# Windowed attention with a highway layer: q and k in half as many transfers, the bias by another queue, one part of q ahead of a weight matrix

## The chip, the cores and the metric

The kernel runs on one core of one Trainium2 chip. A core has five engines that run their own instruction streams in order: TensorE (PE, matmuls; its weight loads are shown as PEld), VectorE (DVE), ScalarE (ACT), GpSimd (POOL) and SyncE (SP). SP, ACT and POOL also issue DMA transfers; all of these run on the core's 16 DMA engines. The metric is the device time of one execution in microseconds (us), lower is better.

## The reference

The inputs are q, k and v of shape (4 batches, 8 heads, 768 positions, 64), and a highway layer's weights w_h and w_t (512 x 512) and bias b_t. Everything is float32 and the output is 3072 x 512.

```python
scores = scale * np.matmul(q, k.transpose(0, 1, 3, 2))
keep = (pos[None, :] < 4) | ((rel >= 0) & (rel < 128))    # 4 sinks, a window of 128
a = softmax(np.where(keep, scores, -1e9))
x = np.matmul(a, v)  # heads side by side: (4 * 768, 512)
H = np.maximum(x @ w_h, 0.0)
T = 1.0 / (1.0 + np.exp(-(x @ w_t + b_t)))
out = T * H + (1.0 - T) * x
```

A query sees itself, the 127 keys before it, and the first four keys of its sequence.

## The kernel before

The work is cut into N = 24 tiles of 128 positions, six for each batch, and each tile carries all eight heads. Tile n needs the keys of its own 128 positions against the queries of tiles n and n + 1, so that one exponential serves both tiles that see these keys.

**Loading.** q and k come as float32 and are needed as float16, cut into segments: three thirds of 256 positions for batches 0 and 1, two halves of 384 for batches 2 and 3. `load_part(b, i, g, which)` (L113) loads, for a group g of two heads, one segment i of q (which = 0) or k (which = 1) into 32 of the 128 partitions of `nat`, with a cast on the way, by POOL's queue; `load_rows` (L122) calls it for the four groups. So each segment of q or k is four transfers of 32 x 2 rows. The first two thirds of q of batch 0 come uncast, as `first`, by the queues of SP and ACT (L180, L197), and are cast by an engine. DVE's `transpose_qk` (L126, L133) turns `nat` into `tr`, from which the products are made. v comes by SP (`load_v`, L137) as float32 with eight buffers, and is cast by `cast_v` (L149) on DVE for tiles 0 to 5 and on POOL from 6 on. w_h and w_t come by POOL with a cast; so does the bias b_t, into `brow`, four rows of 512 at partitions 0, 32, 64 and 96, where a small matmul (L372) adds it to the gate's sum.

**A tile.** `opening` (L387) writes the masks (L309) and the products (L334) of tile n into `ps_s`, of which there is one, with the bias (L372) and the sinks (L380) of earlier tiles in between. ACT takes the exponential into `E` (`expo`, L422). `values(n - 1)` (L433, L436) multiplies E by v, DVE divides (`norm`, L444 and L446) into X, PE transposes X (L462), ACT copies it (L467). Then come the gate (`gate`, L472; `tanh`, L480), the hidden layer (L493), and the combination on DVE (L506, L511) and POOL or DVE (L517), and SP stores the tile.

**What sets the order.** Each engine's order is that of the program text (`_keep_traced_order`, L24). The loop over n (L597) interleaves the stages of tiles n, n - 1 and n - 2. What is loaded, cast and turned in which iteration is written out by hand: `units` (L548) says which segments are turned in iteration n, `loads` (L560) which parts are issued on POOL, `v_at` (L564) which tiles of v are issued on SP; below iteration 6 a load of v waits for the last product of that iteration's scores (`after`, L611). The bf16 and fp16 matmuls at the start and in iterations 0 and 1 (`idle`, L521) work on zeros. On POOL the order at the start is: the first third of k (four parts), the second third of k, the bias (L206), w_t (L207), the last third of q, the last third of k, the copy and product of the sink values (L291, L292), one part of q of batch 1, w_h (L593), and then the loop's.

Of the kernel before, what the change touches and what calls it, by code (L numbers as in the profile page):

```python
# [11 lines left out]
FP32 = mybir.dt.float32  # L12
# [25 lines left out]
def kernel(  # L38
# [13 lines left out]
    P = 128  # L52
    pe, act, dve, pool, sp = nc.tensor, nc.scalar, nc.vector, nc.gpsimd, nc.sync

    B, H, S, D = q.shape
# [5 lines left out]
    NT, DM = out.shape  # L61
# [4 lines left out]
    G = 4  # L66
    HG = H // G
# [4 lines left out]
    const = ctx.enter_context(tc.tile_pool(name="const", bufs=1))  # L72
# [22 lines left out]
    def gate_of(n, part):  # L95
# [6 lines left out]
    segments = [thirds if b < 2 else halves for b in range(B)]  # L102
    nat = [[data.tile([P, 2, HG, nt // 32, D], FP16, tag=f"nat{b}_{t0}", name=f"nat{b}_{t0}")
            for t0, nt in segments[b]] for b in range(B)]
# [5 lines left out]
    def v_of(n):  # L110
        return vt[n % 8]

    def load_part(b, i, g, which, into=None, engine=pool):  # L113

        t0, nt = segments[b][i]
        into = nat[b][i][:, which] if into is None else into
        engine.dma_start(  # L117
            out=into[32 * g:32 * g + 32].rearrange("p hg m d -> p hg (m d)"),
            in_=(q, k)[which][b, :, t0:t0 + nt, :].rearrange(
                "(hg g) (r m) d -> g r hg (m d)", g=G, m=nt // 32)[g])  # L120

    def load_rows(b, i, which, gs=range(G)):  # L122
        for g in gs:
            load_part(b, i, g, which)

    def transpose_qk(b, i, which, hgs=slice(0, HG)):  # L126

# [9 lines left out]
    def load_v(n, after=None):  # L137
        b, t = divmod(n, NC)
        V32[n] = work.tile([P, H, D], FP32, tag="V32", name="V32", bufs=8)
        ins = sp.dma_start(out=V32[n],  # L140
                           in_=v[b, :, t * P:(t + 1) * P, :].transpose([1, 0, 2]))
        if after is not None:
            tc.add_manual_dep(
                ins.ins, after.ins.name,
                mybir.DependencyInfo(
                    mybir.DependencyClass.Sync, mybir.DependencyReason.DATA),
                reason="behind the loads needed first")

    def cast_v(n, engine):  # L149
        engine.tensor_copy(out=v_of(n)[:, :, 0:D], in_=V32[n])  # L150
# [14 lines left out]
    wh = const.tile([P, KC, DM], FP16, tag="wh")  # L165
    wt = const.tile([P, KC, DM], FP16, tag="wt")
    brow = const.tile([P, DM], FP16, tag="brow")
    ones = const.tile([P, P], FP16, tag="ones")
    vs32 = const.tile([P, B, D + 1], FP32, tag="vs32")
    vmask = const.tile([P, H], FP32, tag="vmask")  # L170
# [7 lines left out]
    first = [data.tile([P, HG, SEG // 32, D], FP32, tag=f"first{i}", name=f"first{i}")  # L178
             for i in range(2)]
# [3 lines left out]
    def load_sinks(b, gs=range(G)):  # L183
        for g in gs:
            hs = slice(G * (g // 2), G * (g // 2) + G)
            sp.dma_start(out=vs32[16 * g:16 * g + 16, b, 0:D], in_=v[b, hs, 0:NSINK, :])

    dve.memset(zeros, 0.0)
    dve.memset(brow, 0.0)
    pool.iota(away, pattern=[[1, K2]], base=0, channel_multiplier=-4,  # L190
              allow_small_or_imprecise_dtypes=True)
    load_rows(0, 0, 1)
    for g in range(G):
        pool.iota(vmask[32 * g:32 * g + 32, :], pattern=[[-NSINK, H]], base=0,
                  channel_multiplier=1, allow_small_or_imprecise_dtypes=True)
# [3 lines left out]
    load_v(0)  # L199
    load_v(1)  # L200
    load_sinks(0, range(2, G))
    make_identity(nc, ident)
    load_rows(0, 1, 1)


    pool.dma_start(out=brow[0:P:32, :], in_=moe_b_t.unsqueeze(0).to_broadcast([G, DM]))  # L206
    pool.dma_start(out=wt, in_=moe_w_t.rearrange("(kc p) of -> p kc of", p=P))  # L207
    load_rows(0, 2, 0)
    load_rows(0, 2, 1)

    dve.memset(ebias, _EXP_BIAS)
    for g in range(1, G):
        m = away[32 * g:32 * g + 32, :]
# [76 lines left out]
    def sink_values(b):  # L290
        pool.tensor_copy(out=vs32[64:P, b, 0:D], in_=vs32[0:64, b, 0:D])  # L291
        pool.tensor_tensor(  # L292
            out=vs[b], in0=vs32[:, b].unsqueeze(1).to_broadcast([P, H, D + 1]),
            in1=vmask.unsqueeze(2).to_broadcast([P, H, D + 1]), op=ALU.mult)
# [123 lines left out]
    def expo(n):  # L418
        c = n % NC
        nq = 2 if c + 1 < NC else 1  # L420
        E[n] = work.tile([P, G, HG, 2 * P], FP16, tag="E", name="E")
        act.activation(out=E[n][:, :, :, 0:nq * P], in_=ps_s[:, :, :, 0:nq * P],  # L422
                       func=AF.Exp, bias=ebias, scale=SCALE)
# [97 lines left out]
    def idle(count):  # L521
        for _ in range(count):
            pe.matmul(ps_h, lhsT=zeros[:, 0:P], rhs=zeros, start=True, stop=True,
                      skip_group_check=True)
# [24 lines left out]
    for b in range(1, B):  # L549
# [3 lines left out]
        else:  # L553
            at = (9, 10, 10, 11, 12, 13, 13, 14) if b == 2 else (15, 16, 16, 17, 18, 19, 19, 20)
            for u, n in enumerate(at):
                i, which, hg = u // 4, u // 2 % 2, u % 2
                units.setdefault(n, []).append((b, i, which, slice(hg, hg + 1)))
    issues = [(b, i, g, which) for b in range(1, B) for i in range(len(segments[b]))
              for which in range(2) for g in range(G)][2 * G:]
    loads = {}  # L560
    for n, count in zip(range(2, 18), [4] * 4 + [3] * 7 + [1] + [3] * 3 + [1]):
        loads[n] = [issues.pop(0) for _ in range(count)]
    assert not issues
    v_at = {1: (2,), 2: (3,), 3: (4,), 4: (5,), 5: (6, 7), 6: (8, 9)}  # L564
# [24 lines left out]
    cast_v(0, dve)  # L589
    sink_keys(0, dve)  # L590
    sink_values(0)
    load_rows(1, 0, 0, range(1))
    pool.dma_start(out=wh, in_=moe_w_h.rearrange("(kc p) of -> p kc of", p=P))  # L593

    idle(18)
    last = N - 1
    for n in range(last):  # L597

        nb, n1 = n - 2, n - 1
        joined = n < 5 or n >= 7  # L600
        before = (n1 if 0 <= n1 < N else None, nb if nb >= 0 else None)
        if n < N:
            after = opening(n, *before) if joined else scores(n)
            expo(n)
            if n in (4, 5):
                gate_value(n - 4)
            if n > NC and n % NC == NC - 1:
                gate_value(n - 3)
            for m in v_at.get(n, ()):
                if m < N:  # L610
                    load_v(m, after if n < 6 else None)  # L611
            if n % NC == 3 and n // NC + 1 < B:
                load_sinks(n // NC + 1)
        if 5 <= n <= 6:
            hidden(1 if n == 5 else 3)
        if n == 0:
            idle(5)
        if not joined:
            opening(None, *before)
        if 0 <= n1 < N:  # L620
            values(n1)
        if n >= 6:
            cast_v(n, pool)
        if NC <= n < N and n % NC == 0:
            sink_keys(n // NC)
        if n == 2:
            load_rows(1, 0, 0, range(1, G))
            load_rows(1, 0, 1)
        for b, i, g, which in loads.get(n, ()):
            load_part(b, i, g, which)  # L630
        if n > NC and n % NC == 1:
            sink_values(n // NC)

        done = list(completed.get(n, ()))
        if n == 6:
            while done:
                complete(done.pop(0))
        turn = list(units.get(n, ()))
        if 5 <= n <= 6:
            diff(1 if n == 5 else 3)  # L640
        if 0 <= n1 < N:
            norm(n1)
        if n == 3:
            transpose_qk(0, 2, 1, slice(1, 2))
        if n == 2:
            transpose_qk(0, 2, 0)
        if n == 1:
            transpose_qk(0, 1, 1)
        if 0 < n < 4:
            cast_v(n, dve)  # L650
        if n == 2:
            transpose_qk(0, 2, 1, slice(0, 1))
        for unit in turn if n != 4 else ():
            transpose_qk(*unit)
        if n == 5:
            cast_v(n, dve)

        if nb >= 0:
            gate(nb)
            tanh(nb)  # L660
        if n == 4:
            hidden(0)
            diff(0)
            transpose_qk(*turn.pop())
            cast_v(n, dve)
        if n == 5:
            gate_value(2)
            hidden(2)
        if n == 1:
            idle(3)  # L670
        if 6 <= n <= N:
            hidden(nb, range(KC // 2))
        if 0 <= n1 < N:
            x_transpose(n1)
            if n in sinks_at:
                sink_scores(*sinks_at[n])
            x_copy(n1)
            if n in sinks_at:
                sink_expo(*sinks_at[n])
            if nb >= N - 4:  # L680
                gate_value(nb)
        if 6 <= n <= N:
            hidden(nb, range(KC // 2, KC))
        if n in ahead:
            gate_value(ahead[n], pool)
        if n == last - 1:
            cast_v(last, pool)
        for m in done[:-1]:
            complete(m)
        if n == 5:  # L690
            diff(2)
        if 6 <= n <= N:
            diff(nb)
        for m in done[-1:] if n < last - 1 else ():
            complete(m)
# [83 lines left out]
```

## Time and profile before

| what | us |
|---|---|
| median of three runs | 108.66 |
| lowest and highest run | 107.71 and 108.89 |
| the profiled execution, its time | 108.7 |
| its span, first to last instruction | 106.7 |
| TensorE busy in the span | 94.7 |
| VectorE, ScalarE, GpSimd busy | 86.4, 80.8, 83.8 |

In the lines below, a group or a timeline row names the engine, the line of the kernel, the operation, what it writes and reads, and how often; a bracket at the end of a row of the timeline says how long the engine was idle before it and what ended that. A row of the waits has the waiting engine and line, what it waited for, the total in us, the times, and the longest. A row of the DMA issues has the queue, the number of issues, KB of each and the median us from issue to landing. The two slices lines show tenths of busy time in 40 equal parts of the span.

### The profile page before, as it was taken

To read this page: it belongs to the slowest core of one execution; us is meant where nothing else is said; L and a number is where in the kernel's file an instruction comes from. 1 tells how busy PE (TensorE), PEld (TensorE's weight loads), DVE (VectorE), ACT (ScalarE), POOL (GpSimd) and SP (SyncE) were. 2 spreads that over 40 slices of the span, in tenths; PEclk is the share of its full clock that TensorE was granted. 3 is DMA by queue.
4 is the path that set the end of the run, shared out by engine and by line. 5 is a ranking of instruction groups with operands and counts; after the bars stand their busy time and mean duration, and the time that the engine had idled before them with its cause. 6 is when DMAs were issued, how large, how long until landed. Compare 5 with 4: busy or idle time off the path is not lost. (4 is left out here: it accounts for less than half of the span.)

```text
span 106.7 us, 4672 instructions
## 1 busy us (share of the span) xinstructions
PE 94.7 (89%) x1960; PEld 53.0 (50%) x1960; DVE 86.4 (81%) x188; ACT 80.8 (76%) x105; POOL 83.8 (79%) x139
## 2 busy tenths in 40 slices
PE   5976885889999997799999999999999999999930
PEld 2323452466454654456655467555655565465610
DVE  6988854657796798879998987899889979998960
ACT  3387677689776788778869997897789978986750
POOL 6898729937849999999999999999777829778000
PEclk9999999999999999999999999999999999999999
DMA  2999999999999998879999998999997763252523
GB/s 77 217 256 213 160 202 239 143 188 210 236 216 202 218 157 244 149 176 268 197 234 270 259 237 211 206 244 200 228 266 186 200 179 115 104 198 83 215 84 114
DMA packets 36388, 20.81 MB, mean 195 GB/s; under 512 B 27020, under 2 KB 32912, under 8 KB 36368
## 3 DMA queue, kind: packets, MB, share of 16 engines
q1 hardware_dynamic: 29216, 13.31, 46.7%
q0 software_dynamic: 6848, 6.82, 41.5%
q10 hardware_dynamic: 304, 0.39, 1.2%
q8 instruction: 15, 0.25, 1.0%
q14 instruction: 5, 0.04, 0.1%
HBM read 21.05 MB, written 6.29 MB: 256 GB/s over the span
## 5 line engine op out<-in xcount | busy, mean ns | idle before, releaser
L422 ACT ACTIVATE E<-ps_s,ebias 128x2048 f16<-128x2048 f32 (+1 forms) x24 | 43.8, 1825 | 11.2 <-PE ps_s L334 10.0
L133 DVE STREAM_TRANSPOSE tr<-nat 128x384 f32<-128x384 f32 (+2 forms) x29 | 26.4, 936 | 2.5 <-DMA nat<-in_q_dram 1.4
L493 PE MATMUL ps_h<-wh,XT 128*128 128x512 f16 (+1 forms) x96 | 27.2, 375 | 0.2 <-DVE DD L506 0.2
L517 POOL TENSOR_TENSOR O<-DD,X 128x512 f32<-128x512 f16 x19 | 22.0, 1164 | 6.3 <-DVE DD L511 4.0
L117 POOL DMA_DIRECT2D nat<-in_k_dram x40 | 21.9, 551 | 3.0 <-DMA wt<-in_moe_w_t_dram 1.9
L472 PE MATMUL ps_z<-wt,XT 128*128 128x512 f16 (+1 forms) x96 | 24.2, 374 | 0.0
L117 POOL DMA_DIRECT2D nat<-in_q_dram x32 | 17.8, 560 | 4.3 <-DMA wh<-in_moe_w_h_dram 2.2
L506 DVE SCALAR_TENSOR_TENSOR DD<-ps_h,X 128x512 f16<-128x512 f32 (+1 forms) x24 | 16.1, 673 | 4.2 <-PE ps_h L493 4.2
L480 ACT ACTIVATE TH<-ps_z 128x512 f16<-128x512 f32 (+1 forms) x24 | 14.0, 583 | 3.6 <-PE ps_z L472 3.6
L446 DVE TENSOR_TENSOR X<-ps_av,rec 128x512 f16<-128x512 f32 x23 | 15.9, 692 | 0.8
L467 ACT COPY XT<-ps_av 128x512 f16<-128x512 f16 x23 | 13.5, 587 | 3.4 <-PE ps_av L355 1.8
L334 PE MATMUL ps_s<-tr 32*64 32x192 f16 (+3 forms) x768 | 13.3, 241 | 2.2 <-DVE tr L133 2.0
L436 PE MATMUL ps_av<-v,E 128*128 128x65 f16 x184 | 13.4, 193 | 1.6 <-POOL v L150 1.3
L433 PEld LDWEIGHTS <-E 128*128 128x128 f16 x160 | 10.4, 97 | 5.5 <-issue 4.5
L433 PE MATMUL ps_av<-v,E 128*128 128x65 f16 x152 | 12.5, 194 | 0.0
L436 PEld LDWEIGHTS <-E 128*128 128x128 f16 x192 | 11.9, 97 | 0.8 <-issue 0.6
L150 POOL CAST v<-V 128x512 f16<-128x512 f32 x18 | 12.1, 669 | 0.0
L493 PEld LDWEIGHTS <-XT 128*128 128x128 f16 x100 | 8.8, 98 | 6.6 <-issue 0.4
L334 PEld LDWEIGHTS <-tr 32*64 32x64 f16 x768 | 10.3, 104 | 3.1 <-issue 1.7
L511 DVE TENSOR_TENSOR DD<-DD,TH 128x512 f16<-128x512 f16 (+1 forms) x23 | 10.4, 456 | 0.8
L472 PEld LDWEIGHTS <-XT 128*128 128x128 f16 x100 | 8.2, 98 | 5.7 <-issue 0.2
L462 PEld LDWEIGHTS <-X 128*128 128x128 f16 x96 | 5.9, 97 | 9.6 <-DVE X L446 8.7
(90 smaller groups left out, 113.9 us busy)
## 6 DMA issues: line engine op xcount, KB each, us to landing
V<-in_v_dram SPq DMA_DIRECT2D x24, 256.0 KB, 5.6
out_dram<-O SPq DMA_DIRECT2D x23, 256.0 KB, 3.4
nat<-in_k_dram POOLq DMA_DIRECT2D x24, 64.0 KB, 5.3
nat<-in_q_dram POOLq DMA_DIRECT2D x16, 96.0 KB, 4.7
nat<-in_k_dram POOLq DMA_DIRECT2D x16, 96.0 KB, 4.6
nat<-in_q_dram POOLq DMA_DIRECT2D x16, 64.0 KB, 5.7
first<-in_q_dram SPq DMA_DIRECT2D x6, 128.0 KB, 3.6
wt<-in_moe_w_t_dram POOLq DMA_DIRECT2D x1, 512.0 KB, 7.3
```

The lines of the kernel that those rows point to most:

```text
L117: engine.dma_start(out=into[32 * g:32 * g + 32].rearrange("p hg m d -> p hg (m d)"), in_=(q, k)[which][b, :, t0:t0 + nt, :].rearrange("(hg ...
L133: dve.transpose(out=dst, in_=src)
L334: return pe.matmul(ps_s[ks, g, hg, q0:q1], lhsT=tr[b][rows, 1, hg, k0:k0 + K2, e], rhs=tr[b][rows, 0, hg, c * P + q0:c * P + q1, e], start ...
L422: act.activation(out=E[n][:, :, :, 0:nq * P], in_=ps_s[:, :, :, 0:nq * P], func=AF.Exp, bias=ebias, scale=SCALE)
L433: pe.matmul(slot, lhsT=E[n - 1][:, g, hg, P:2 * P], rhs=v_of(n - 1)[:, h, :], start=first, stop=False, skip_group_check=True)
L436: pe.matmul(slot, lhsT=E[n][:, g, hg, 0:P], rhs=v_of(n)[:, h, :], start=first, stop=True, skip_group_check=True)
L446: dve.tensor_tensor(out=X[n], in0=av[:, :, :, 0:D], in1=rec.unsqueeze(3).to_broadcast([P, HG, G, D]), op=ALU.mult)
L472: pe.matmul(into, lhsT=XT[n][:, kc * P:(kc + 1) * P], rhs=wt[:, kc, cols], start=False, stop=(kc == KC - 1), skip_group_check=True)
L480: act.activation(out=TH[n][:, cols], in_=ps_z if z is None else z, func=AF.Tanh, scale=0.5)
L493: pe.matmul(into, lhsT=XT[n][:, kc * P:(kc + 1) * P], rhs=wh[:, kc, cols], start=(kc == 0), stop=(kc == KC - 1), skip_group_check=True)
L506: dve.scalar_tensor_tensor(out=DD[n][:, cols], in0=ps_h[:, cols] if h is None else h, scalar=0.0, in1=flat(X[n], cols), op0=ALU.max, op1=A ...
L517: eng.tensor_tensor(out=O[n][:, cols], in0=DD[n][:, cols], in1=flat(X[n], cols), op=ALU.add)
```

## The change

Four things change together.

1. For batches 1 to 3, `load_heads` takes the place of `load_part`: one transfer brings one segment of q or k for half of the heads (four heads, hg = 0 or 1) into all 128 partitions. A segment is two transfers of 128 rows, not four of 64. The loop issues them on a new list, and in iterations 3 to 5 they wait for the last product of that iteration's scores.
2. The bias comes as float32 by SP's queue into a new tile, behind the sink loads, and ACT casts it into `brow` right after the exponential of tile 0.
3. On POOL one of the four parts of batch 0's last third of q is issued ahead of w_t; the bias is gone from there.
4. w_h is issued ahead of batch 1's first q, of which both transfers follow it before the loop.

`behind` holds what `load_v` did for a wait on `after`; `load_rows` is gone, its calls written out.

```diff
+    def behind(ins, after):
+        if after is not None:
+            tc.add_manual_dep(
+                ins.ins, after.ins.name,
+                mybir.DependencyInfo(
+                    mybir.DependencyClass.Sync, mybir.DependencyReason.DATA),
+                reason="behind the loads needed first")
...
-    def load_rows(b, i, which, gs=range(G)):
-        for g in gs:
-            load_part(b, i, g, which)
+    def load_heads(b, i, hg, which, after=None):
+
+        t0, nt = segments[b][i]
+        ins = pool.dma_start(
+            out=nat[b][i][:, which, hg].rearrange("p m d -> p (m d)"),
+            in_=(q, k)[which][b, :, t0:t0 + nt, :].rearrange(
+                "(hg g) (r m) d -> hg g r (m d)", g=G, m=nt // 32)[hg])
+        behind(ins, after)
...
+    brow32 = const.tile([P, DM], FP32, tag="brow32")
...
-    dve.memset(brow, 0.0)
+    dve.memset(brow32, 0.0)
...
     load_sinks(0, range(2, G))
+    sp.dma_start(out=brow32[0:P:32, :], in_=moe_b_t.unsqueeze(0).to_broadcast([G, DM]))
     make_identity(nc, ident)
-    load_rows(0, 1, 1)
-    pool.dma_start(out=brow[0:P:32, :], in_=moe_b_t.unsqueeze(0).to_broadcast([G, DM]))
+    for g in range(G):
+        load_part(0, 1, g, 1)
+    load_part(0, 2, 0, 0)
     pool.dma_start(out=wt, in_=moe_w_t.rearrange("(kc p) of -> p kc of", p=P))
-    load_rows(0, 2, 0)
-    load_rows(0, 2, 1)
+    for g in range(1, G):
+        load_part(0, 2, g, 0)
+    for g in range(G):
+        load_part(0, 2, g, 1)
...
-    issues = [(b, i, g, which) for b in range(1, B) for i in range(len(segments[b]))
-              for which in range(2) for g in range(G)][2 * G:]
+    issues = [(b, i, hg, which) for b in range(1, B) for i in range(len(segments[b]))
+              for which in range(2) for hg in range(HG)][HG:]
-    for n, count in zip(range(2, 18), [4] * 4 + [3] * 7 + [1] + [3] * 3 + [1]):
+    for n, count in enumerate([2] * 5 + [2, 1, 1] * 4, 2):
...
-    load_rows(1, 0, 0, range(1))
     pool.dma_start(out=wh, in_=moe_w_h.rearrange("(kc p) of -> p kc of", p=P))
+    for hg in range(HG):
+        load_heads(1, 0, hg, 0)
...
             expo(n)
+            if n == 0:
+                act.copy(out=brow, in_=brow32)
...
-        if n == 2:
-            load_rows(1, 0, 0, range(1, G))
-            load_rows(1, 0, 1)
-        for b, i, g, which in loads.get(n, ()):
-            load_part(b, i, g, which)
+        for b, i, hg, which in loads.get(n, ()):
+            load_heads(b, i, hg, which, after if 3 <= n <= 5 else None)
```

More of the change, by code (lines that the diff above doesn't have):

```diff
@@ L141, in load_v @@
                            in_=v[b, :, t * P:(t + 1) * P, :].transpose([1, 0, 2]))
[L142 to L147, printed above, removed]
+        behind(ins, after)
     def cast_v(n, engine):
@@ L188 @@
     dve.memset(zeros, 0.0)
-    dve.memset(brow, 0.0)
+    dve.memset(brow32, 0.0)
     pool.iota(away, pattern=[[1, K2]], base=0, channel_multiplier=-4,
               allow_small_or_imprecise_dtypes=True)
-    load_rows(0, 0, 1)
+    for g in range(G):
+        load_part(0, 0, g, 1)
     for g in range(G):
@@ L201 @@
     load_sinks(0, range(2, G))
+    sp.dma_start(out=brow32[0:P:32, :], in_=moe_b_t.unsqueeze(0).to_broadcast([G, DM]))
     make_identity(nc, ident)
-    load_rows(0, 1, 1)
-    pool.dma_start(out=brow[0:P:32, :], in_=moe_b_t.unsqueeze(0).to_broadcast([G, DM]))
+    for g in range(G):
+        load_part(0, 1, g, 1)
+    load_part(0, 2, 0, 0)
     pool.dma_start(out=wt, in_=moe_w_t.rearrange("(kc p) of -> p kc of", p=P))
-    load_rows(0, 2, 0)
-    load_rows(0, 2, 1)
+    for g in range(1, G):
+        load_part(0, 2, g, 0)
+    for g in range(G):
+        load_part(0, 2, g, 1)
     dve.memset(ebias, _EXP_BIAS)
```

## The prediction

> **What bounds the kernel now.** First the page's head, engine line and slices, to see where TensorE is not full.
>
> ```profile
> span 106.7 us, 4672 instructions
> PE 94.7 (89%) x1960; PEld 53.0 (50%) x1960; DVE 86.4 (81%) x188; ACT 80.8 (76%) x105; POOL 83.8 (79%) x139
> ...
> PE   5976885889999997799999999999999999999930
> ...
> PEclk9999999999999999999999999999999999999999
> DMA  2999999999999998879999998999997763252523
> ```
>
> A slice is 2.67 us. PE is full from the tenth slice on, but for two (40 to 45 us) and the tail; its holes are in the first 24 us. The DMA engines are busy from the second slice on, so a transfer asked for early waits behind others. Next, who waited for whom, and the timelines of PE, DVE and ACT over the front.
>
> ```profile
> PE ps_s L334 <- DVE tr L133: 2.0, 2, 1.5
> ...
> PE ps_av L436 <- POOL v L150: 1.3, 2, 0.8
> ```
>
> ```profile
> 1.19 5.96 PE L523 MATMUL ps_h<-zeros 128*128 128x512 f16 x18 [1.19 <-DVE zeros L188]
> ...
> 13.13 0.40 PE L462 MATMUL ps_av<-ident,X 128*128 128x128 f16 x4 [0.38 <-DVE X L446]
> 13.70 0.32 PE L309 MATMUL ps_s<-mq,mk 32*64 32x256 bf16 x8 [0.18 <-ACT E L422]
> ...
> 16.60 0.40 PE L462 MATMUL ps_av<-ident,X 128*128 128x128 f16 x4 [0.24 <-DVE X L446]
> ...
> 19.06 0.56 PE L334 MATMUL ps_s<-tr 32*64 32x192 f16 x32 [1.47 <-DVE tr L133]
> ...
> 21.88 0.40 PE L462 MATMUL ps_av<-ident,X 128*128 128x128 f16 x4 [0.59 <-DVE X L446]
> ...
> 23.18 0.20 PE L433 MATMUL ps_av<-v,E 128*128 128x65 f16 x1
> ```
>
> ```profile
> 17.91 1.10 DVE L133 STREAM_TRANSPOSE tr<-nat 128x512 f32<-128x512 f32 x1 [1.37 <-DMA nat<-in_q_dram]
> ...
> 20.42 0.65 DVE L133 STREAM_TRANSPOSE tr<-nat 128x256 f32<-128x256 f32 x1 [0.79 <-DMA nat<-in_k_dram]
> ```
>
> ```profile
> 8.71 1.97 ACT L422 ACTIVATE E<-ps_s,ebias 128x2048 f16<-128x2048 f32 x1 [1.06 <-issue]
> 11.68 1.97 ACT L422 ACTIVATE E<-ps_s,ebias 128x2048 f16<-128x2048 f32 x1 [1.00 <-PE ps_s L334]
> ...
> 14.77 1.97 ACT L422 ACTIVATE E<-ps_s,ebias 128x2048 f16<-128x2048 f32 x1 [0.62 <-PE ps_s L334]
> ```
>
> The largest hole is at tile 3: the third q lands, DVE transposes it from 17.91, and PE, idle for 1.47, gets its scores at 19.06. The third k then holds DVE until 20.42, and with it the norm behind. Later PE waits twice, 1.3 us in all, for a cast of v that POOL makes late. The whole front is one chain, exponential to scores to exponential, since a single ps_s is read by ACT (8.71, 11.68, 14.77) before PE may write it again (13.70 stands right behind 11.68 + 1.97).
>
> **The change, part by part.** (1) Transfers by half of the heads. POOL's issues and two later exponentials:
>
> ```profile
> L117 POOL DMA_DIRECT2D nat<-in_k_dram x40 | 21.9, 551 | 3.0 <-DMA wt<-in_moe_w_t_dram 1.9 <-issue 0.5 <-DMA nat<-in_k_dram 0.4
> ...
> L207 POOL DMA_DIRECT2D wt<-in_moe_w_t_dram x1 | 0.8, 805 | 0.0
> ```
>
> ```profile
> 51.32 0.62 POOL L150 CAST v<-V 128x512 f16<-128x512 f32 x1
> ...
> 77.18 1.15 POOL L517 TENSOR_TENSOR O<-DD,X 128x512 f32<-128x512 f16 x1 [0.70 <-issue]
> ```
>
> ```profile
> 55.52 1.97 ACT L422 ACTIVATE E<-ps_s,ebias 128x2048 f16<-128x2048 f32 x1 [0.61 <-PE ps_s L334]
> ...
> 76.38 1.97 ACT L422 ACTIVATE E<-ps_s,ebias 128x2048 f16<-128x2048 f32 x1 [0.62 <-PE ps_s L334]
> ```
>
> Batches 1 to 3 have 56 POOL issues and get 28. One of 64 rows takes 551 ns, w_t's of 512 rows 805, so 128 rows cost about 0.59 us: 30.9 us becomes 16.5, and POOL gives up some 14 us. Almost none is on PE's path. Batch 2's six tiles take 76.38 - 55.52 = 20.86 us with PE full and POOL never waiting; from 77.18 POOL does wait, and PE is no fuller for it. Only the two late casts count: -1.3 us (bounds 0 and -1.3; POOL gets about 0.9 us more room in each tile from 7 on, and its casts stand behind fewer issues, so I take it all). The issues that now wait for scores in tiles 3 to 5 hold nothing: POOL has no cast there, only loads. Those loads go out one tile later and are needed two or three tiles on: no cost.
>
> (2) The bias. It leaves POOL (one issue) for SP, behind the last two sink loads, and its cast stands on ACT between the exponentials of tiles 0 and 1. All that follows on ACT waits for its landing.
>
> ```profile
> 6.27 2.82 SPq L186 DMA_DIRECT2D vs<-in_v_dram  x2
> ...
> 14.76 5.29 SPq L140 DMA_DIRECT2D V<-in_v_dram  x2
> ```
>
> ```profile
> first<-in_q_dram SPq DMA_DIRECT2D x6, 128.0 KB, 3.6
> ...
> brow<-in_moe_b_t_dram POOLq DMA_DIRECT2D x1, 4.0 KB, 5.5
> ```
>
> ```profile
> V<-in_v_dram SPq DMA_DIRECT2D x1, 256.0 KB, 7.5
> ```
>
> ```profile
> L581 ACT CAST nat<-first 128x512 f16<-128x512 f32 x1 | 0.6, 620 | 0.7 <-DMA first<-in_q_dram 0.7
> ```
>
> SP is through with the sinks at 6.27 + 2.82 = 9.09. Landing takes 3.6 us on SP before the engines fill, 7.5 for the next v (issued at 11.68); the bias itself took 5.5 on POOL's queue. I take 5.5, the same four rows into the same stage: landed at 14.6 (bounds 12.7 and 16.6). The cast takes 0.62 (L581's size), so the exponential of tile 1 starts at 15.2, not 11.68: 3.5 late. Its slack was 1.0, ACT's wait in that row, and that would hide the cast only if the bias were there by about 11.1. The larger memset of the FP32 row costs nothing: DVE waits for the first q after it.
>
> Carried down the chain: exponential 2 at 18.3; the transposes of x at 16.60 move to 20.1; DVE turns the third q right behind the norm at about 20.0 and ends at 21.1. Scores 3 start at 21.1 against 19.06: +2.05, since 1.47 of the 3.5 was waited for already. The third k is there by then, which gives 0.4 back at the norm (DVE's 20.42 wait): +1.65 at scores 4.
>
> (3) Then v. SP issues tile 3's v behind scores 2 (14.76, now 18.3), and tile 4's behind scores 3.
>
> ```profile
> V<-in_v_dram SPq DMA_DIRECT2D x1, 256.0 KB, 5.2
> ```
>
> ```profile
> V<-in_v_dram SPq DMA_DIRECT2D x1, 256.0 KB, 8.1
> ```
>
> ```profile
> 15.33 0.54 POOL L117 DMA_DIRECT2D nat<-in_k_dram  x1 [1.86 <-DMA wt<-in_moe_w_t_dram]
> ...
> 17.83 0.77 POOL L593 DMA_DIRECT2D wh<-in_moe_w_h_dram  x1
> ...
> 24.54 2.24 POOL L117 DMA_DIRECT2D nat<-in_q_dram  x4 [2.17 <-DMA wh<-in_moe_w_h_dram]
> ```
>
> The first row is tile 3's v, which went ahead of w_h (17.83) and landed in 5.2; the second is tile 4's, behind w_h and batch 1, in 8.1. Tile 3's v now stands where tile 4's stood: 7.5, nearer the second, so 25.8, cast by 26.2. Values 3, at 23.18 before, would want it at 24.85: another +1.35 (bounds 0 and 2), +3.0 in all. Tile 4's v had cost PE about 0.2, which goes, as its landing has room: +2.8 for the front.
>
> (4) A part of the third q ahead of w_t. POOL keeps eight transfers in flight: the last third k waits for w_t and is the eighth behind it, as the issue at 24.54 is the eighth behind w_h. The bias gone and one q part before w_t, the last k waits for that part and goes out near 13, not 15.33. Third q, still behind w_t but for a quarter, lands perhaps 0.5 earlier, third k 1.5. In the chain above both are early already: 0 here (bounds 0 and -0.6); without (2) it would be the gain.
>
> The profiled execution took 108.7 us around its span of 106.7, at the median of the runs. Sum: 108.7 + 2.8 - 1.3 = **110.2**.
>
> **Rivals.** *The bias lands in time* (the other side; by about 11.1, and up to 12.5 it costs little, as tile 3 waited 1.47 anyway). Then third q at 17.3 and third k give -0.6 at tile 3 and after, tile 4's v -0.2, POOL -1.3: 106.6. For it: four rows are little, and q's transfers took 3.6 on this queue. Against: 64 KB behind or 4 KB, all took over 5 in this stage. Chance 0.28.
>
> *Late transposes.* The new source starts with a dimension of four heads, where each old transfer started with 32 rows. If a transfer is dealt out over that dimension it lies on four of 16 engines.
>
> ```profile
> q0 software_dynamic: 6848, 6.82, 41.5%
> ```
>
> ```profile
> nat<-in_q_dram POOLq DMA_DIRECT2D x16, 96.0 KB, 4.7
> ```
>
> ```profile
> 57.22 0.85 DVE L133 STREAM_TRANSPOSE tr<-nat 128x384 f32<-128x384 f32 x1
> ```
>
> A packet of this queue takes 0.415 x 106.7 x 16 / 6848 = 0.103 us, so 32 in a row on one engine are 3.3 us where 8 were 0.8: landing 4.7 becomes at least 7.2. Tile 10's loads follow its cast (51.32 + 0.62, some 0.8 sooner now); the transpose is at 57.22: 6.1 us of room. DVE would stall about 1.1 on the first; as each stall gives the next load room, a third of it stays, some 0.35 in each of nine tiles: 3 us, 113.2. Decides from a landing of 6.1 on. No row shows a transfer like it on POOL's queue. Chance 0.2. The Trainium skill ("DMA: Bandwidth & Descriptors", "Rules for kernel authors") states just this, that an outermost dimension of c under 16 confines a DMA to at most c engines, though its section on the semaphore increment of 16 has an exception for some copies of this queue; by the rule the sum would be 113.2, by the landing rows 110.2.
>
> *A cold TensorE.* In my chain PE idles from 13.53 to 17.2 (15.2 + 1.97), 3.7 us; its longest wait here is 1.47.
>
> ```profile
> 97.95 0.86 PE ps_z L472 x4
> ```
>
> At the start 18 matmuls of 512 columns took 5.96 us where four in step later take 0.86: 2.1 us of slow start, though the granted clock is printed as full. If the gap brings that back while PE has work for some three fifths of the time, 1.3: 111.5. Chance 0.1. The Trainium skill ("TensorE: Matmul & The Clock Gate", "Part 1: The HAM clock gate") says so: half rate after an idle window of about 3.4 us; a free-running window that a 3.7 us gap need not cover is why I keep it a rival, and no row of this trace shows such a gap.
>
> **How the numbers follow.** Main case 0.42, at 110.2. Its own range: with the bias at 12.7 the front moves by 1.6 - 1.47 - 0.4 - 0.2, about -0.4, and with no wait for v the sum is 107.0; with 16.6 by 5.5 - 1.47 - 0.4 - 0.2 + 2 = +5.4, which gives 112.8. Range: from the case in time, 106.5, to 112.8, which leaves out most of the late transposes and little else. A measurement of this kernel tells about 1% from no change, 107.6 to 109.8. Faster: most of 0.28, 0.26. Within 1%: its rest and a third of the main case, 0.16. Slower: 0.58.
>
> **What would show it.** Right: ACT's row of the bias cast stands behind a DMA wait of over 3 us, the exponential of tile 1 near 15; DVE's cast of tile 3's v waits for its DMA; POOL has idle time in every tile and PE no wait for a cast of v. Wrong: a bias cast that waits under 1 us; q and k transfers of over 7 us with DVE's transposes waiting for them; matmuls twice as long behind the gap; or a hole at tile 3 that is still there at 1.47.

## The result, and the profile after

| | us |
|---|---|
| after, median of 6 runs (lowest, highest) | 119.19 (117.03, 122.92) |
| before, median of 6 runs on the same chip | 109.03 (107.71, 110.97) |
| ratio after to before, 95% interval | 1.084 [1.067, 1.102] |
| the profiled execution of after, its span | 118.51, 116.7 |

The change makes the kernel 8.4% slower. The forecast was 110.2, with a range from 106.5 to 112.8: the direction was right, the size was not. Ratios here compare undisturbed runs only, so they can differ a little from the quotient of two medians; e2_early below had one such run and so has no ratio, and the profiles of e2_early, e4_heads_only, e5_parts_cast1 and e6_flat_cast1 were taken in disturbed ones (that of e4_heads_only at 120.68 us, where its other three runs took 115.72 to 116.48).

The page of after: head, busy row, the slices, POOL's queue.

```profile
span 116.7 us, 4623 instructions
...
PE 98.2 (84%) x1960; PEld 53.6 (46%) x1960; DVE 86.0 (74%) x188; ACT 81.1 (70%) x106; POOL 72.7 (62%) x110
...
PE   5976639979999999989699759988799858999950
...
PEclk9999976999999999999999999999999999999996
...
q0 software_dynamic: 17120, 6.86, 43.2%
```

POOL is busy 11 us less, where some 14 were forecast: one of the 28 issues takes 0.70 us and not 0.59. TensorE now has holes all through the second half, where before it stood at 9. POOL's queue moves the same 6.8 MB in 17120 packets, not 6848. The waits of after, and its DMA issues (KB of one, us to landing):

```profile
POOL O L532 <- DVE DD L526: 17.6, 13, 3.3
...
DVE tr L147 <- DMA nat<-in_k_dram: 9.5, 7, 2.6
...
ACT brow L622 <- DMA brow<-in_moe_b_t_dram: 2.8, 1, 2.8
...
DVE tr L147 <- DMA nat<-in_q_dram: 1.8, 2, 1.2
```

```profile
nat<-in_q_dram POOLq DMA_DIRECT2D x8, 192.0 KB, 8.2
nat<-in_k_dram POOLq DMA_DIRECT2D x8, 192.0 KB, 8.2
```

The transposes (L133 before) now wait 11.3 us for q and k; a transfer takes 8.2 us to land, where one of half the size took 4.7. All but 0.5 us of these waits are for batches 2 and 3: eight of their 16 transposes wait, 10.9 us in all. No wait of PE for a cast of v by POOL is left. To see where the time went, read the start of ACT's exponential for tiles 1, 6, 10 and 23 from its timeline; the first rows of after are

```profile
9.13 1.97 ACT L437 ACTIVATE E<-ps_s,ebias 128x2048 f16<-128x2048 f32 x1 [1.45 <-PE ps_s L349]
...
13.87 0.62 ACT L622 CAST brow<-brow 128x512 f16<-128x512 f32 x1 [2.78 <-DMA brow<-in_moe_b_t_dram]
14.39 1.96 ACT L437 ACTIVATE E<-ps_s,ebias 128x2048 f16<-128x2048 f32 x1
```

and the table gives the same for all kernels of this study, in us of one profiled execution each. A tile's column is the start of its exponential, and "6 to 10" is the time from tile 6's to tile 10's:

| kernel | tile 1 | tile 6 | 6 to 10 | 10 to 23 |
|---|---|---|---|---|
| before | 11.68 | 31.73 | 16.91 | 45.26 |
| after | 14.39 | 34.72 | 15.20 | 54.05 |
| e4_heads_only (parts 1 and 4) | 12.03 | 36.03 | 15.18 | 54.86 |
| e3_parts (parts 2 and 3) | 15.29 | 35.44 | 15.45 | 45.23 |
| e1_flat (source begins with 128) | 15.59 | 35.78 | 15.44 | 45.91 |
| e8_eight (source begins with 8) | 14.85 | 34.74 | 15.59 | 47.37 |
| e9_two (source begins with 2) | 14.88 | 39.97 | 16.64 | 46.61 |
| e2_early (issued earlier) | 15.60 | 35.67 | 15.44 | 48.28 |
| e5_parts_cast1 | 12.43 | 32.69 | 15.44 | 45.23 |
| e6_flat_cast1 | 12.36 | 35.17 | 15.18 | 45.81 |
| e7_parts_warm | 14.61 | 35.83 | 15.44 | 45.56 |
| b1_bias_first | 12.06 | 31.69 | 16.22 | 45.20 |
| b3_bias_first_q_behind | 12.15 | 33.01 | 16.11 | 45.19 |

After against before: +3.0 at tile 6, -1.7 from there to tile 10, +8.8 from tile 10 to 23. The sum, 10.1, is the whole difference (the spans differ by 10.0). The last term is the one that the prediction missed, and this is how it looks. POOL's timeline of after, then DVE's, with all eight waits:

```profile
47.32 1.15 POOL L532 TENSOR_TENSOR O<-DD,X 128x512 f32<-128x512 f16 x1 [1.22 <-DVE DD L526]
48.42 0.60 POOL L159 CAST v<-V 128x512 f16<-128x512 f32 x1
48.98 0.70 POOL L134 DMA_DIRECT2D nat<-in_k_dram  x1
51.62 1.15 POOL L532 TENSOR_TENSOR O<-DD,X 128x512 f32<-128x512 f16 x1 [1.94 <-DVE DD L526]
```

```profile
49.51 0.85 DVE L147 STREAM_TRANSPOSE tr<-nat 128x384 f32<-128x384 f32 x1 [1.22 <-DMA nat<-in_q_dram]
...
53.53 0.86 DVE L147 STREAM_TRANSPOSE tr<-nat 128x384 f32<-128x384 f32 x1 [0.38 <-DMA nat<-in_k_dram]
...
57.37 0.85 DVE L147 STREAM_TRANSPOSE tr<-nat 128x384 f32<-128x384 f32 x1 [0.97 <-DMA nat<-in_k_dram]
...
61.15 0.87 DVE L147 STREAM_TRANSPOSE tr<-nat 128x384 f32<-128x384 f32 x1 [0.59 <-DMA nat<-in_q_dram]
...
67.37 0.86 DVE L147 STREAM_TRANSPOSE tr<-nat 128x384 f32<-128x384 f32 x1 [2.57 <-DMA nat<-in_k_dram]
...
79.59 0.87 DVE L147 STREAM_TRANSPOSE tr<-nat 128x384 f32<-128x384 f32 x1 [1.77 <-DMA nat<-in_k_dram]
...
91.11 0.86 DVE L147 STREAM_TRANSPOSE tr<-nat 128x384 f32<-128x384 f32 x1 [1.18 <-DMA nat<-in_k_dram]
95.83 0.84 DVE L147 STREAM_TRANSPOSE tr<-nat 128x384 f32<-128x384 f32 x1 [2.17 <-DMA nat<-in_k_dram]
```

The stalls go up and down, and the last is among the longest: they don't die out. The issue at 48.98 stands behind a combination that waits for DVE's DD, so when DVE stalls on a transpose, DD can be late, and with it POOL's next issue.

### The profile page after: what moved, and what is told of

Read it like the earlier page. It is cut to its first block, busy times and chain, and to the rows that moved or that the text cites. A ratio compares the mean times of both kernels' runs of the same rounds, so it can differ in the third digit from the quotient of the medians.

```text
span 116.7 us, 4623 instructions
## 1 busy us (share of the span) xinstructions
PE 98.2 (84%) x1960; PEld 53.6 (46%) x1960; DVE 86.0 (74%) x188; ACT 81.1 (70%) x106; POOL 72.7 (62%) x110
## 3 DMA queue, kind: packets, MB, share of 16 engines
q0 software_dynamic: 17120, 6.86, 43.2%
## 4 chain that ended last, share of the span: by engine, by line
DMA 39%; PE 30%; POOL 11%; issue 8%; DVE 6%; ACT 2%; POOLq 0%; DVEq 0%
DMA nat<-in_k_dram 18%; PE ps_h L508 8%; DMA nat<-in_q_dram 7%; PE ps_z L487 7%; DMA V<-in_v_dram 7%; DMA brow<-in_moe_b_t_dram 4%; PE ps_s L349 3%; DMA out_dram<-O 3%; POOL O L532 3%; POOL nat L134 3%; POOL v L159 3%; DVE tr L147 2%; PE ps_av L448 2%; PE ps_av L451 2%; PE ps_av L477 2%
## 5 line engine op out<-in xcount | busy, mean ns | idle before, releaser
L147 DVE STREAM_TRANSPOSE tr<-nat 128x384 f32<-128x384 f32 (+2 forms) x29 | 27.0, 937 | 11.6 <-DMA nat<-in_k_dram 9.5
L532 POOL TENSOR_TENSOR O<-DD,X 128x512 f32<-128x512 f16 x19 | 21.8, 1152 | 21.8 <-DVE DD L526 17.6
L487 PE MATMUL ps_z<-wt,XT 128*128 128x512 f16 (+1 forms) x96 | 24.7, 378 | 0.3 <-issue 0.3
L349 PE MATMUL ps_s<-tr 32*64 32x192 f16 (+3 forms) x768 | 14.7, 246 | 4.0 <-DVE tr L147 2.4
L451 PE MATMUL ps_av<-v,E 128*128 128x65 f16 x184 | 13.9, 196 | 0.5 <-DVE v L159 0.5
L134 POOL DMA_DIRECT2D nat<-in_q_dram x14 | 9.8, 704 | 5.0 <-PE ps_s L349 5.0
L477 PE MATMUL ps_av<-ident,X 128*128 128x128 f16 x92 | 9.0, 220 | 3.8 <-DVE X L461 3.7
L134 POOL DMA_DIRECT2D nat<-in_k_dram x14 | 9.9, 709 | 1.8 <-PE ps_s L349 1.8
```

The costliest lines, as they stand in the source:

```text
L134: ins = pool.dma_start(out=nat[b][i][:, which, hg].rearrange("p m d -> p (m d)"), in_=(q, k)[which][b, :, t0:t0 + nt, :].rearrange("(hg g) ...
L147: dve.transpose(out=dst, in_=src)
L349: return pe.matmul(ps_s[ks, g, hg, q0:q1], lhsT=tr[b][rows, 1, hg, k0:k0 + K2, e], rhs=tr[b][rows, 0, hg, c * P + q0:c * P + q1, e], start ...
L451: pe.matmul(slot, lhsT=E[n][:, g, hg, 0:P], rhs=v_of(n)[:, h, :], start=first, stop=True, skip_group_check=True)
L477: pe.transpose(xt[:, kc // 2, (kc % 2) * P:(kc % 2 + 1) * P], x[:, kc * P:(kc + 1) * P], ident)
L487: pe.matmul(into, lhsT=XT[n][:, kc * P:(kc + 1) * P], rhs=wt[:, kc, cols], start=False, stop=(kc == KC - 1), skip_group_check=True)
```

## The experiments

Parts are numbered here as in the section on the change. My theory after the result: a transfer whose source begins with a dimension of four heads lies on four of the 16 DMA engines, lands in 8 us, and stalls DVE. Rivals: that the transfers are half as many and twice as large, or that they are issued later; and, for the front, the place of the bias cast against a slow TensorE. Line numbers differ a little between the kernels.

**e1_flat.** The transfers keep size, number, place and target, but the source is 128 rows that lie one behind another in memory, so that a single dimension of 128 comes first. It attends over wrong keys.

```diff
-            in_=(q, k)[which][b, :, t0:t0 + nt, :].rearrange(
-                "(hg g) (r m) d -> hg g r (m d)", g=G, m=nt // 32)[hg])
+            in_=(q, k)[which][b].rearrange("h s d -> (h s) d")[
+                hg * G * S + t0:hg * G * S + t0 + G * nt, :].rearrange(
+                "(p m) d -> p (m d)", p=P))
```

> The changed kernel with one thing different: each transfer of load_heads reads 128 rows that lie one behind the other in q or k, so that its source begins with a dimension of 128 and not of four heads; bytes, rows, destination, order and waits stay (it reads other rows of q and k, so the attention is over wrong keys). Theory of four engines: a transfer whose source begins with four lies on four DMA engines; here it lies on 16, landing falls from 8.2 us to 5 or 6, POOL's queue falls from 17120 packets to about 6400, DVE's waits for nat (11.3 us) fall under 2, and the time to 109.5 to 111, that is the front's 2.9 us over the kernel before less POOL's 1.3. Rival, size: a transfer of twice the rows lands late on any number of engines; then landing stays over 7 us and the time over 116. Rival, position: the new list simply issues too late; then the waits for nat stay too.

Measured: 111.16 us, ratio 1.026 [1.017, 1.035], 0.2 above what was expected. Its queue row and issues:

```profile
q0 software_dynamic: 6368, 6.82, 39.9%
```

```profile
nat<-in_q_dram POOLq DMA_DIRECT2D x8, 192.0 KB, 5.5
nat<-in_k_dram POOLq DMA_DIRECT2D x8, 192.0 KB, 5.4
```

The same bytes by the same number of transfers land in 5.4 to 5.5, and tiles 10 to 23 take 45.9, not 54.05. Of the 16 transposes of batches 2 and 3 one waits, for 0.9 us. So neither the number nor the size of the transfers costs the 8 us, nor the place of their issue; the source does. Its rows now also lie in one piece; that this is not what helps is shown by e8_eight below, whose source is in more pieces than that of after and yet lands earlier.

**e2_early.** Each load goes out an iteration earlier from iteration 6 on.

```diff
-    for n, count in enumerate([2] * 5 + [2, 1, 1] * 4, 2):
+    for n, count in enumerate([2] * 4 + [4] + [1, 1, 2] * 3 + [1, 1], 2):
```

> The changed kernel with the transfers of batches 2 and 3 issued one iteration earlier (from iteration 6 on, not 7). If only latency is at fault (8.2 us against some 6 of room), one iteration of 3.5 us more room takes DVE's waits for nat to under 2 us and the time to 109.5 to 111.5. If the transfers on few engines also take each other's and v's place, landing grows and a good part of the waits stays: 112 to 116. If size or engines had nothing to do with it and the loss lay elsewhere, nothing changes: 117 to 119.

Measured: median 114.8 of 4 runs, 112.18 to 116.22; all lie below the lowest run of after, 117.03. From its waits and its issues:

```profile
DVE tr L147 <- DMA nat<-in_k_dram: 1.2, 1, 1.2
```

```profile
nat<-in_q_dram POOLq DMA_DIRECT2D x8, 192.0 KB, 9.3
```

Landing stays bad and the stalls of batches 2 and 3 are gone: the one wait that is left is for batch 0, at 7.98 us. What hurts is landing against the room that a load has. The time came out where the second theory had it, but its sign, waits that stay, did not. Tiles 10 to 23 still take 3.0 more than before (48.28 to 45.26). A part of it is a stall of PE that the profile puts down to "issue" (1.9 us at 60.12); what that was, and the rest, stays open.

**e3_parts.** Parts 1 and 4 undone (`load_part`, `issues`, the counts and the start of batch 1 as before, w_h behind the first q of batch 1); the bias by SP, its cast behind tile 0's exponential, and the part of q ahead of w_t stay.

> The changed kernel with its first part undone: q and k of the later batches come by quarters again, on the old list and with w_h behind the first of them; the bias by SP with its cast on ACT, and the part of the third q ahead of w_t, stay. If the bias costs what the front shows, ACT waits for it and tile 6's exponential stays 2 to 3 us behind the kernel before: 111 to 112 us. If the late front came from the transfers of batch 1 and not from the bias, the front recovers and it is 108 to 109.

Measured: 110.72 us, 1.025 [1.016, 1.034]. Two of its waits, and its row of the stretch from 14 to 20 us, in which the two numbers after the engines' busy times are the granted clock and the DMA share:

```profile
PE ps_s L328 <- ACT E L441: 4.4, 2, 3.5
...
ACT brow L625 <- DMA brow<-in_moe_b_t_dram: 3.7, 1, 3.7
```

```profile
14.00:20.00 6.00, 2.70 (x61) 2.06 (x61) 0.71 (x3) 4.50 (x4) 5.26 (x10) 0.67 1.03 164
```

Parts 2 and 3 alone make the kernel 2.5% slower, all of it ahead of tile 6 (+3.7). And 6 to 10 is 1.5 shorter than before with all 56 issues back on POOL, and no wait for a cast of v: fewer issues are not what removed it. That a later front gives POOL's casts their time is only argued.

**e4_heads_only.** The kernel before with part 1, and part 4 with it (w_h ahead of batch 1's first q).

> The kernel before with the first part alone: transfers by half of the heads on the new list, w_h ahead of them; bias and third q as before. Four engines: DVE waits some 9 to 11 us for nat, the front is that of the kernel before: 115 to 117 us. If the loss needs the late front as well (the bias and the transfers together), it is under 112.

Measured: 116.17 us, 1.073 [1.064, 1.081]. Tiles 10 to 23 take 54.86, as in after: parts 2 and 3 are not needed for it. Part 4 isn't the cause, since e1_flat has it too and takes 45.91. In this profile tile 6 also starts 4.3 us late, as a q of batch 1 lands late in a front that is on time. But the profile's span is 12.2 us over before, while the ratio stands for some 8; that those 4.3 us belong to the change is not shown. DVE's timeline, then PE's:

```profile
29.61 1.10 DVE L150 STREAM_TRANSPOSE tr<-nat 128x512 f32<-128x512 f32 x1 [3.33 <-DMA nat<-in_q_dram]
```

```profile
31.01 0.19 PE L453 MATMUL ps_av<-v,E 128*128 128x65 f16 x1 [2.97 <-DVE v L167]
```

**e8_eight and e9_two.** A dose: the source begins with eight heads of 16 rows, or two of 64. Both attend over wrong keys.

```diff
-            in_=(q, k)[which][b, :, t0:t0 + nt, :].rearrange(
-                "(hg g) (r m) d -> hg g r (m d)", g=G, m=nt // 32)[hg])
+            in_=(q, k)[which][b, 0:8, 0:16 * (nt // 32), :].rearrange(
+                "h (r m) d -> h r (m d)", m=nt // 32))
```

> The changed kernel with the same bytes and destination, but each transfer reads 16 rows of all eight heads, so that its source begins with a dimension of eight (wrong keys for half of the rows). Theory that the engines follow the first dimension: data on eight engines, 16 rows each; in the changed kernel POOL's queue has 17120 packets, which is 5920 and 28 times 400, and 400 is 12 idle engines times 32 and 16; so here 28 times (8 x 16 + 16) and 5920 = 9952 packets, landing 6 to 7 us, time 110 to 114. If the four engines come from something else (128 partitions, the size), packets stay at 17120 or fall to 6368.

> The changed kernel with each transfer reading 64 rows of two heads (wrong keys for most rows): its source begins with a dimension of two. By the rule that fits 4, 8 and 128 so far, data on two engines and 14 x 64 + 16 = 912 small packets for each of 28 transfers: 5920 + 28 x 912 = 31456 packets on POOL's queue, landing 12 us or more, and a time above 122 us. If four is a floor of the queue, packets stay at 17120.

Measured: e8_eight 112.3 us and e9_two 117.76 us, one run each. The queue and the issues of e8_eight:

```profile
q0 software_dynamic: 9952, 6.83, 42.6%
```

```profile
nat<-in_q_dram POOLq DMA_DIRECT2D x8, 192.0 KB, 6.4
```

9952 - 6368 = 28 x 8 x 16, and 17120 - 6368 = 28 x 12 x 32: for each of the 28 transfers, as many extra packets as idle engines times rows on a busy one, for eight and for four engines. Landing goes 5.5, 6.4, 8.2 with 16, 8, 4, and tiles 10 to 23 take 45.9, 47.4, 54.05. Eight pieces of 16 rows land sooner than four of 32, so it is not the number of pieces that makes them late.

e9_two came out at 17120 packets again, not 31456. The DMA view of it for 14 to 45 us, for 60 to 116 us, and its issues:

```profile
q0 software_dynamic: 12644, 2.44, 69.4%
```

```profile
q0 software_dynamic: 1734, 2.37, 26.7%
```

```profile
nat<-in_k_dram POOLq DMA_DIRECT2D x8, 192.0 KB, 5.6
...
nat<-in_k_dram POOLq DMA_DIRECT2D x6, 128.0 KB, 11.0
```

The 12 transfers of 192 KB in the second stretch take 1734 / 12 = 144 packets each, as in e1_flat: by the same count these lie on all 16 engines; they land in 5.6, and tiles 10 to 23 cost only 46.6. The extra packets all belong to batch 1's transfers, which land in 10 to 11, behind which a v arrives late (DVE waits 4.8 us for it) and tile 6 starts at 39.97. The edit itself says why the two sizes differ. For a segment of 384 positions it reads 64 rows of 12 from each head, which is all 768 positions, so the second head follows the first without a gap and the source is 128 equal steps, as in e1_flat. For a segment of 256 it reads 64 rows of 8, 512 of 768, and two heads stay two pieces. Then the rule fits to the packet: 17120 - 6368 = 12 x 14 x 64, the 12 transfers of batch 1 with 14 idle engines and 64 rows on a busy one. That after has the same total (28 x 12 x 32) is chance, and no sign that four engines are the least. No view shows the dimensions of a transfer, so that the two are taken as one is inferred from the 144 packets. It is a test within one kernel: where the packets multiply the time goes, and where they don't it doesn't. Whether the fewer engines make a transfer late, or the extra packets that come with them, no run separates.

**e5_parts_cast1, e6_flat_cast1.** e3_parts, and e1_flat, with ACT's bias cast one exponential later.

```diff
-            if n == 0:
+            if n == 1:
                 act.copy(out=brow, in_=brow32)
```

> e3_parts with ACT's cast of the bias one tile later, behind the exponential of tile 1. The bias lands near 13.8 us and that exponential ended at 13.65 in the kernel before, so ACT no longer waits: E of tile 1 near 12, TensorE's gap under 1.5 us, granted clock full, third q and third k earlier than before. Theory that the wait at the cast is the whole loss of e3_parts: 107 to 108.5 us, at or below the kernel before. Rival, that the third q ahead of w_t or the order at SP costs by itself: 109.5 to 111.

> e1_flat (128 rows one behind the other, wrong keys) with the cast behind the exponential of tile 1: the change without its two faults. If the two explain all of the loss: 106.5 to 108.5 us, with the front of e5_parts_cast1 and no late cast of v. If fewer and larger transfers cost something besides the engines they lie on, it stays above e5_parts_cast1 by over 1 us.

Measured: 107.76 us, 0.986 [0.973, 0.999] for e5; 109.25 us, 1.002 [0.996, 1.008] for e6. A single place in ACT's order is worth 3.9% between e3 and e5, and 2.4% between e1 and e6. In e5 ACT still waits 0.9 us for the bias, and the clock was not full (0.74 from 14 to 20 us), against what was expected. e6 came out above its 106.5 to 108.5: larger transfers on 16 engines gain nothing here. It stands at 27.18 at tile 5, the same as before, and then waits. DVE's timeline of e6:

```profile
29.67 0.43 DVE L160 CAST v<-V 128x512 f16<-128x512 f32 x1 [2.35 <-DMA V<-in_v_dram]
```

w_h and batch 1 went out earlier (w_h at 16.06, not 17.83), and tile 4's v landed behind them. That the one made the other late is argued; e1_flat has such a wait too (2.2 us). The span of this profile is 2.2 us over before, the ratio 1.002, so not every execution need have the whole of it.

**e7_parts_warm.** e3_parts with 14 more matmuls on zeros in the gap, to tell a slow clock from the wait itself.

```diff
             x_copy(n1)
+            if n == 1:
+                idle(14)
```

> e3_parts with 14 more matmuls on zeros in TensorE's gap, behind the transposes of tile 0's x. They take 3 us of a 3.5 us gap and delay nothing. If the low granted clock behind the gap (0.67 from 14 to 20 us in e3_parts) costs the front 1 to 2 us by itself: 108.8 to 109.9 us and a clock of 1.0 throughout. If matmuls there are hidden behind ACT's exponentials and the third k, the time stays at 110.3 to 111.

Measured: 111.6 us, 1.017 [1.000, 1.034]; not the 108.8 to 109.9 expected. The exponential of tile 3 comes 2.4 earlier than in e3 (20.91, not 23.33), of which 0.7 was there at tile 1 already. The granted clock is 1.00 from 14 to 20 us, not 0.67, so slow matmuls were part of that loss; but a v then lands late (DVE's cast waits 2.09 at 25.52), and tile 6 starts no sooner than in e3. Inconclusive for the time.

**b1_bias_first, b3_bias_first_q_behind.** b1 is e3_parts with the bias issued by ACT's queue behind its first loads; b3 is b1 with all of the third q behind w_t.

```diff
     dve.memset(brow32, 0.0)
+    act.dma_start(out=brow32[0:P:32, :], in_=moe_b_t.unsqueeze(0).to_broadcast([G, DM]))
...
-    sp.dma_start(out=brow32[0:P:32, :], in_=moe_b_t.unsqueeze(0).to_broadcast([G, DM]))
```

> e3_parts (q and k by quarters, one part of the third q ahead of w_t) with the bias issued by ACT's queue right behind its two first loads of q, ahead of all of v, and its cast behind the exponential of tile 0 as in the change. The bias lands by about 6 us, so the cast finds it there and takes 0.6 us of ACT's 1.0 us of waiting: tile 1's exponential no later than in the kernel before, the third q and third k 0.5 and 1.5 us earlier. Theory that only the landing of the bias was wrong with the second part: 106.5 to 108 us, at or below e5_parts_cast1 and 1 to 2% below the kernel before. Rival, that the early front is taken back by v of tiles 3 and 4, which lands behind w_h: 108 to 109.

> b1_bias_first with the third q wholly behind w_t again, so that only the bias is moved against the kernel before. If the part of q ahead of w_t earns what b1_bias_first gains, through the last third k that goes out near 13 and not 15.3 us, this one loses it again: the hole at tile 3 is back at some 1.5 us and the time 0.5 to 1.5 us above b1_bias_first. If the gain comes from the bias leaving POOL's queue, both are equal.

Measured: b1 107.55 us, 0.987 [0.980, 0.993], 1.3% below before and the fastest of this study with e5; b3 108.43 us, 1.000 [0.996, 1.004]. So the bias on ACT's queue, with its cast on ACT, is worth nothing by itself. ACT's timeline of b1:

```profile
10.95 0.61 ACT L625 CAST brow<-brow 128x512 f16<-128x512 f32 x1
12.06 1.97 ACT L441 ACTIVATE E<-ps_s,ebias 128x2048 f16<-128x2048 f32 x1 [0.51 <-PE ps_s L353]
```

The cast fits into the slack ahead of tile 1 once the bias is there. What remains of the change's gain is then the part of q ahead of w_t, 1.3%. It does not come at tile 3, as was expected: PE's hole there is 1.55 us in b1 and gone in b3, and the exponential starts at 20.12 in b1 and 18.61 in b3. It comes later: in b3 tile 4's v lands late. DVE's timeline of b3:

```profile
29.05 0.45 DVE L163 CAST v<-V 128x512 f16<-128x512 f32 x1 [1.88 <-DMA V<-in_v_dram]
```

## Why the prediction was wrong

The numbers in brackets are those of the prediction's parts.

**(1) Transfers by half of the heads: the failed step.** The sum gave them -1.3 us, with a landing as before (4.7 us), and put the late transposes aside as a rival with a chance of 0.2 and a price of 3 us. The landing was 8.2 us. The late transposes cost 8.8 us between tiles 10 and 23: the table shows 54 to 55 us there with part 1 (54.05, 54.86) and not without it or with its source laid flat (45.23, 45.91). With only the source laid flat, the change measured 2.6% over before, where the forecast was 1.4%; so most of the miss is this step. Two things were mis-judged:

- The chance. "No row shows a transfer like it on POOL's queue" was true, and the landing rows of other shapes were then taken as the nearest. The rule of the Trainium skill ("DMA: Bandwidth & Descriptors", "Rules for kernel authors") that the prediction quoted says that an outermost dimension of 4 leaves at most four engines; packets and landing (8.2, 6.4 and 5.5 us with 4, 8 and 16) agree with it, and the exception on the same page did not show for sources that begin with 2, 4 or 8. That the data are on exactly four engines is read from packet counts; no view lists a transfer's engines.
- The size. The rival had a landing of at least 7.2 us (7.6 by its own working, as its 4.7 belongs to transfers of 64 rows, 4 and not 8 on an engine), a first stall of 1.1, and then let two thirds of each die out, "as each stall gives the next load room": 0.35 us for each load. Eight transposes waited 1.36 us each on average, 10.9 in all. The room did grow, but not enough. At the eight waits DVE was ready for the transfer 6.6 to 8.3 us after the start of its issue, against the 6.1 of the prediction, and began the transpose 7.7 to 10.1 us after it. e2_early gives more room, and these stalls go with the landing as long as ever. That the issuer is itself behind DVE, through the combination, is a reason why the stalls last, but its weight is not shown: POOL waits 17.6 us for DD in after and 4.0 before, yet from 48 to 97 us it also waits 9.6 in e1_flat, which takes only 0.7 more than before from tile 10 to 23, and 11.6 in after. POOL's wait before:

```profile
POOL O L517 <- DVE DD L511: 4.0, 5, 2.0
```

That the waits for POOL's casts would go was right (-1.7 measured, -1.3 forecast), but not its reason: e3 shows the same (-1.5) with 56 issues.

**(2) and (3), the bias and the v behind it: right, in place and nearly in size.** ACT waited 2.8 us for the bias, just short of the 3 that was named as the sign. Landing 13.9 (forecast 14.6), exponential of tile 1 at 14.39 (15.2), tile 3's v cast at 25.22 with a wait (26.2), +3.0 at tile 6 (+2.8). A small part of this is luck: the bias came 0.7 sooner, and by the exponential of tile 3 the lead was gone (21.64, and 19.68 + 2.05 by the forecast). Slow matmuls took back at least a part of it. PE's timeline of after:

```profile
16.41 0.44 PE L324 MATMUL ps_s<-mq,mk 32*64 32x256 bf16 x8 [2.56 <-ACT E L437]
...
18.72 1.35 PE L487 MATMUL ps_z<-wt,XT 128*128 128x512 f16 x4
```

Without that slow stretch, those four matmuls take 1.02 us in the same kernel. e5 and b1 show from the other side that ACT's wait for the bias is the whole cost: with most or all of it gone, parts 2 and 3 of the change are a gain of 1.3 to 1.4%.

**(4) The part of q:** that it is worth 0 with the bias late no run tests. "Without (2) it would be the gain" was right in sign: 1.3%, some 1.4 us, between b1 and b3. The path was another. For that case the prediction had 0.6 us from the third q and k at tile 3 and 0.2 from tile 4's v; the gain shows at tile 4's v and not at tile 3.

**The cold TensorE** (chance 0.1) came on top of the others, with a granted clock of 0.72 from 14 to 20 us. Its share in after is not settled: e7 took 1.7 us back between tiles 1 and 3 and lost them to a late v.

**w_h ahead of batch 1's q** (part 4 of the change) was no term of the sum, and no run has it alone or leaves it out alone.

## What to carry to other kernels

Before transfers are merged, look at which dimension comes first in the source: with four heads in front the same bytes landed in 8.2 us that landed in 5.5 with 128 rows in front, and the queue's packet count (17120 against 6368) told it at once. Compare a load's landing with its room, and don't count on stalls to die out: here eight of 16 loads came late, to the last one. A cast that waits for a small, late transfer stops all that follows on its engine; the cast one place further back, or the transfer issued earlier on another queue, turned a loss of 2.5% into a gain of 1.3 to 1.4%.

## What the runs showed of the hardware

- A transfer that leaves engines out still costs packets on them: 28 transfers of 128 rows made 6368 packets when flat, 9952 with eight heads in front and 17120 with four. The issue on POOL grows too, from about 0.56 us (flat) to 0.70.
- Two heads in front need not mean two pieces: where the rows read are the whole of each head, e9 has the 144 packets a transfer of e1_flat, and otherwise the most extra packets of all (896) and a landing of 10 to 11 us.
- SP's transfers get slower as well in after: in the issues view, v's landing goes from 5.6 us to 7.0, and the output's from 3.4 to 4.3; in e1_flat they are 5.6 and 3.4 again, in e8 5.9 and 3.8.
- In e6, e7 and b3 tile 3 comes earlier than in the kernel each was made from (by 3.7, 2.4 and 1.5 us), and in each DVE then waits about 2 us for a v of tile 3 or 4. But e5, earlier than e3 by 2.6 us, has no such wait, and e1_flat has one (2.2 us) without being early. What makes that v late no run isolates.
- The granted clock can fall without a long gap. In e3, a wait of 3.5 us and 0.67 agree with the Trainium skill ("TensorE: Matmul & The Clock Gate", "Part 1: The HAM clock gate"), which names an idle window of about 3.4 us. But after shows 0.72 behind 2.56 us, and e5, in which no wait of PE from 11 to 24 us is over 0.87 us, has 0.74 between 14 and 20 us, and is faster than before all the same. What set the clock there stays open. The rows of after and of e5:

```profile
14.00:20.00 6.00, 3.59 (x64) 2.30 (x63) 2.18 (x5) 4.80 (x4) 4.34 (x6) 0.72 1.00 166
```

```profile
14.00:20.00 6.00, 5.02 (x103) 3.03 (x108) 3.42 (x7) 4.18 (x6) 4.73 (x8) 0.74 1.22 211
```
